# Sorted attention plus routed experts: heads in pairs, a smaller sort matrix, and expert work issued between the attention stages

## The chip, the cores and the metric

One core of one Trainium2 chip. The metric is the device time of one execution in microseconds (us), median over several runs, lower is better.

## The reference, cut to what matters

```python
# attention: batch 4, heads 8, seq 768, head_dim 64, 8 blocks of 96
for _ in range(5):                       # Sinkhorn on sort_net, [32, 8, 8]
    P = exp(P - max);  P /= rows;  P /= columns
k_sorted[i] = sum_j P[i, j] * k_block[j]; v_sorted likewise
attn = softmax(q_block @ k_sorted.T / 8);  o = attn @ v_sorted
x = o as [3072, 512]
# experts: E = 8, D = 512, F = 1024
G = exp(x @ w_gate);  8 Sinkhorn rounds on G [3072, 8]
out = sum_e G[:, e] * (relu(x @ w1[e]) @ w2[e])
```

Every token goes through every expert. That is 8 x 6 chunks of 512 tokens x (32 + 32) matmuls of 512 columns: 3072 in all, in both kernels.

## The kernel before

One head at a time. P goes to memory and comes back spread over the partitions; a sort matrix R of 128 x 2304 is built per head, and twelve matmuls of 384 columns sort k and v together. The expert part comes after the attention.

```python
    Pdr = dram.tile([32, 8, 8], F32)
    nc.sync.dma_start(out=Pdr, in_=P)
    Pbig2 = pp.tile([128, 32, 8], F32)
    for j in range(8):
        nc.gpsimd.dma_start(out=Pbig2[16 * j:16 * (j + 1), :, :], in_=...)      # cut
    ...
    for g in range(NH):                                   # 32 heads
        ktv = iop.tile([128, 6, 128], BF16, name="ktv")   # k | v
        ... three loads, 96 KB each ...
        R = rp.tile([128, 2, 6, 4, 96], BF16, name="R")
        for nh in range(2):
            for i2 in range(4):
                nc.vector.tensor_scalar(out=outap, in0=mask, scalar1=Pbig2[:, g, i:i + 1], ...)
        for nh in range(2):
            for kk in range(6):
                nc.tensor.matmul(sortps[:, nh, 0:384], ktv[:, kk, :], R[:, nh, kk],
                                 start=(kk == 0), stop=(kk == 5))
        ... 8 q transposes, 8 scores, exp, 8 v transposes, 8 products, normalise ...
    ...
    for e in range(E):
        for nc4 in range(6):
            ... 32 matmuls hps, 8 Relu on ACT, 32 matmuls oacc, 4 accumulations on DVE ...
```

The softmax here doesn't subtract the row's maximum and nothing guards it: scores larger than these inputs give would overflow.

## Time and profile before

| | before |
|---|---|
| device time | 852.1 us (848.5 to 855.5, 16 runs) |
| first sort matmul | 27.45 us |
| first expert matmul | 172.9 us |
| last matmul ends | 845.1 us |
| span | 849.3 us |

The four times are read off the timeline: rows give the start, the length, the engine, the source line, the operation with output and inputs, and the idle time before it with what ended it. The page's fourth part and the list of stretches say which of them is on the path. The lines themselves stand in the prediction.

### The profile page before, as it was taken

The page shows a single profiled execution, that of the slowest core. Times are in us where ns is not written, and L with a number is a line of the kernel's source. Part 1 is how long each engine was busy: PE and PEld are TensorE (multiplying, and loading weights), DVE is VectorE, ACT ScalarE, POOL GpSimd, SP SyncE. Part 2 cuts the span into 40 slices and gives each one's busy share as a digit, 9 for nine tenths or more (in the row PEclk, how much of TensorE's full clock was granted, in tenths as well). Part 3 has the DMA queues.
Part 4 walks back from the last instruction along what each step waited for, and adds up shares of the span by engine and source line. Part 5 has one row for each costly group of instructions (what it writes and reads, how often), then busy time and mean ns, then how long its engine had stood idle before and what let it go on. Part 6 is the DMA issues. An engine that isn't in the chain of part 4 may idle for free.

```text
span 849.3 us, 11251 instructions
## 1 busy us (share of the span) xinstructions
PE 797.7 (94%) x4657; PEld 402.4 (47%) x4720; DVE 283.7 (33%) x603; ACT 333.8 (39%) x543; POOL 99.6 (12%) x131
## 2 busy tenths in 40 slices
PE   0678999998999999999999999999999999999997
PEld 0456777753444444444444444444444444444443
DVE  4758888655222222212121212122221212121212
ACT  1357777742333333242424233333324242424332
POOL 4745555300000000000000000000000000000000
PEclk9999999999999999999999999999999999999999
DMA  8999999600006000600060005001400000001212
GB/s 117 124 166 102 71 71 71 44 1 1 1 1 99 1 1 1 100 0 1 1 100 0 1 5 95 0 1 25 75 1 0 1 1 1 0 1 50 100 55 94
DMA packets 92419, 33.52 MB, mean 39 GB/s; under 512 B 76768, under 2 KB 85200, under 8 KB 92368
## 3 DMA queue, kind: packets, MB, share of 16 engines
q0 software_dynamic: 88592, 26.36, 30.2%
q1 hardware_dynamic: 3776, 6.44, 2.1%
q8 instruction: 37, 0.61, 0.3%
q14 instruction: 14, 0.11, 0.1%
HBM read 52.58 MB, written 6.30 MB: 69 GB/s over the span
## 4 chain that ended last, share of the span: by engine, by line
PE 88%; DMA 4%; DVE 3%; ACT 3%; issue 1%; POOL 1%; ACTq 0%
PE oacc L276 39%; PE hps L268 38%; PE sortps L157 7%; ACT kvTs L170 2%; PE tps L191 2%; DMA ktv<-in_k_dram 1%; PE scps L177 1%; DMA ktv<-in_v_dram 1%; PE ogps L201 1%; POOL Pbig L72 1%; DMA Pdr<-P 1%; PE csps L253 0%; DVE cs L252 0%; DMA qg<-in_q_dram 0%; PE ggps L238 0%
## 5 line engine op out<-in xcount | busy, mean ns | idle before, releaser
L271 ACT ACTIVATE hTs<-hps 128x512 bf16<-128x512 f32 x384 | 229.1, 597 | 424.5 <-PE hps L268 404.1
L276 PE MATMUL oacc<-w2e,hTs 128*128 128x512 bf16 x1506 | 339.3, 380 | 3.5 <-DVE osbl L279 1.7
L268 PE MATMUL hps<-xtT,w1e 128*128 128x512 bf16 x1503 | 338.1, 379 | 1.7
L283 DVE SCALAR_TENSOR_TENSOR osbl<-oacc,glog,osbl 128x512 f32<-128x512 f32 x168 | 126.1, 751 | 454.0 <-PE oacc L276 432.4
L276 PEld LDWEIGHTS <-hTs 128*128 128x128 bf16 x1536 | 150.8, 98 | 183.6 <-issue 4.0
L268 PEld LDWEIGHTS <-w1e 128*128 128x128 bf16 x1536 | 150.2, 98 | 179.4
L150 DVE TENSOR_SCALAR R<-mask,Pbig 128x576 bf16<-128x576 bf16 x256 | 92.8, 419 | 21.3 <-DMA Pbig<-Pdr 12.2
L157 PE MATMUL sortps<-R,ktv 128*128 128x384 bf16 x384 | 78.1, 335 | 12.7 <-ACT kvTs L170 6.4
L103 POOL DMA_DIRECT2D w1e<-in_moe_w_dram x8 | 6.1, 762 | 399.1 <-PE hps L268 399.1
L157 PEld LDWEIGHTS <-ktv 128*128 128x128 bf16 x384 | 35.1, 100 | 34.0 <-issue 11.9
L166 PE MATMUL tps<-I,qg 96*96 96x96 bf16 x256 | 17.5, 211 | 26.9 <-DMA qg<-in_q_dram 26.9
L170 ACT CAST kvTs<-sortps 128x768 bf16<-128x768 f32 x32 | 25.5, 798 | 41.2 <-PE sortps L157 41.2
L279 DVE TENSOR_SCALAR osbl<-oacc,glog 128x512 f32<-128x512 f32 x24 | 17.8, 750 | 46.9 <-PE oacc L276 45.4
L184 ACT ACTIVATE atp<-scps 96x768 bf16<-96x768 f32 x32 | 25.8, 806 | 19.4 <-PE scps L177 18.3
L140 POOL DMA_DIRECT2D ktv<-in_k_dram x32 | 26.7, 835 | 55.2 <-PE sortps L157 43.6
L166 PEld LDWEIGHTS <-qg 96*96 96x96 bf16 x256 | 15.7, 127 | 28.1 <-issue 27.0
L141 POOL DMA_DIRECT2D ktv<-in_v_dram x32 | 26.4, 826 | 0.0
L142 POOL DMA_DIRECT2D qg<-in_q_dram x32 | 25.9, 809 | 0.1
L172 ACT COPY qTs<-tps 96x768 bf16<-96x768 bf16 x32 | 25.5, 795 | 0.1
L208 DVE TENSOR_TENSOR ogallP<-ogps,recips 96x512 bf16<-96x512 f32 x32 | 21.7, 678 | 0.3
L177 PEld LDWEIGHTS <-kvTs 96*96 96x96 bf16 x256 | 16.8, 126 | 4.7 <-issue 0.8
L195 ACT COPY vsbP<-tps 96x512 bf16<-96x512 bf16 x32 | 18.3, 573 | 0.0
(47 smaller groups left out, 174.0 us busy)
## 6 DMA issues: line engine op xcount, KB each, us to landing
w1e<-in_moe_w_dram POOLq DMA_DIRECT2D x8, 1024.0 KB, 8.1
w2e<-in_moe_w_dram POOLq DMA_DIRECT2D x8, 1024.0 KB, 8.9
out_dram<-osbl SPq DMA_DIRECT2D x24, 256.0 KB, 2.0
ktv<-in_k_dram POOLq DMA_DIRECT2D x32, 96.0 KB, 3.1
ktv<-in_v_dram POOLq DMA_DIRECT2D x32, 96.0 KB, 3.7
qg<-in_q_dram POOLq DMA_DIRECT2D x32, 96.0 KB, 3.5
Pbig<-Pdr POOLq DMA_DIRECT2D x8, 16.0 KB, 2.4
mask<-mask SPq DMA_DIRECT2D x7, 18.0 KB, 5.3
```

Of the source, the lines that this page charges most:

```text
L140: nc.gpsimd.dma_start(out=ktv[:, :, 0:64], in_=kf[g].rearrange("(p kk) d -> p kk d", kk=6))
L141: nc.gpsimd.dma_start(out=ktv[:, :, 64:128], in_=vf[g].rearrange("(p kk) d -> p kk d", kk=6))
L142: nc.gpsimd.dma_start(out=qg[0:96, qb, :, 0:64], in_=qf[g].rearrange("i c d -> c i d"))
L150: nc.vector.tensor_scalar(out=outap, in0=mask, scalar1=Pbig2[:, g, i:i + 1], scalar2=None, op0=ALU.mult)
L157: nc.tensor.matmul(sortps[:, nh, 0:384], ktv[:, kk, :], R[:, nh, kk], start=(kk == 0), stop=(kk == 5),)
L166: nc.tensor.matmul(qTps[0:96, i, :], qg[0:96, qb, i, :], I96, is_transpose=True, start=True, stop=True)
L170: nc.scalar.copy(kvTs, sortps[:, :, 0:384])
L184: nc.scalar.activation(out=atp[0:96], in_=scps[0:96, :, 0:384], func=AF.Exp, scale=scale)
L268: nc.tensor.matmul(hps, w1e[:, kk, fb * 128:(fb + 1) * 128], xtT[:, kk, nc4 * 512:(nc4 + 1) * 512], start=(kk == 0), stop=(kk == 3))
L271: nc.scalar.activation(out=hTs[:, fb, :], in_=hps, func=AF.Relu)
L276: nc.tensor.matmul(oacc, hTs[:, fb, tt * 128:(tt + 1) * 128], w2e[:, fb, :], start=(fb == 0), stop=(fb == 7))
L283: nc.vector.scalar_tensor_tensor(out=osbl[:, t, :], in0=oacc, scalar=glog[:, t, e:e + 1], in1=osbl[:, t, :], op0=ALU.mult, op1=ALU.add)
```

## The change

Its intent: get rid of the trip to memory, make the attention cheap on TensorE, and hand the time that TensorE still idles in it to expert matmuls. Cut to its core:

```diff
-    Pdr = dram.tile([32, 8, 8], F32)                      # P out and back, eight loads
-    ...
+    for _ in range(46):                                   # dummy matmuls, to have the clock up
+        nc.tensor.matmul(w_, wide[:, 0:128], wide, start=True, stop=True)
+    ... Sinkhorn with one max instead of five; the last product writes Prep, P repeated 16 times ...
+    for i in range(8):
+        nc.tensor.matmul(pbp[:, i, :], Prep[:, i]..., ident[0:32, 0:32], start=True, stop=True)
+    def stage1(m):                                        # pair m of heads
+        for src, dic, nm in ((kb, KT, "KT"), (vb, VT, "VT")):
+            for kh2 in range(2):
+                b_ = bank([128, 3, 128])
+                for k3 in range(3):
+                    for h2 in range(2):                   # head 0 -> partitions 0-63, head 1 -> 64-127
+                        nc.tensor.matmul(b_[64 * h2:64 * h2 + 64, k3, :], src[:, h2, 3 * kh2 + k3, :],
+                                         R[:, h2]..., start=True, stop=True)
+                ... KT halves and the first VT half copied by ACT, the second by DVE ...
+        ... 12 q transposes likewise, QT copied by DVE; R of the next pair built (256 columns) ...
+    ... stage2: 16 scores of 64 rows, exp, 8 transposes to VS; stage3: 16 products, normalise;
+        stage4: 8 transposes, copied into xtT by ACT ...
+    for m in range(NPAIR + 4):                            # order of every engine's queue as written
+        stage1(m); fill(1); stage2(m - 1); fill(1); stage3(m - 2); fill(1); gate; stage4(m - 3); fill(1)
+    ... routing rounds with fill(3) each; then y tiles, h blocks up to nine chunks ahead ...
```

`fill(1)` issues one expert block (four matmuls of 512 columns and a Relu), if the batch it needs is through the attention. All PSUM tiles rotate through one pool of eight banks.

## The prediction

> **What bounds the kernel now.** I read the stretches first, cut where the tenths of the engines change. Columns: stretch, length, then busy time and instruction count of PE, PEld, DVE, ACT and POOL, granted TensorE clock, DMA share, GB/s.
>
> ```profile
> 0.00:23.73 23.73, 0.00 (x0) 0.00 (x0) 9.12 (x42) 2.56 (x6) 11.31 (x24) 1.00 0.78 107
> ...
> 80.00:160.00 80.00, 75.00 (x908) 56.76 (x907) 67.52 (x190) 59.03 (x85) 46.45 (x57) 1.00 1.12 72
> ...
> 204.36:849.30 644.94, 637.64 (x2905) 290.13 (x2963) 141.90 (x189) 219.55 (x368) 8.18 (x10) 1.00 0.13 27
> ```
>
> Three quarters of the span is the expert network, TensorE 99% busy. Before it come 24 us without a matmul, then attention at a fixed beat: 57 POOL issues at three a head are 19 heads in 80 us, 4.21 us a head. No expert matmul runs in that stretch.
>
> The chain that ended last, in order of time (start, length, what), gives the speed of the expert part and the cause of the empty start.
>
> ```profile
> 13.84 4.61 DMA Pdr<-P
> 18.73 5.00 POOL Pbig L72 x8
> ...
> 810.57 6.91 PE oacc L276 x32
> ```
>
> Thirty-two 512-column matmuls take 6.91 us, 215.9 ns each. The experts need 3072 of them: 8 experts x 6 chunks x (32 + 32). That is **663.2 us, untouched by the change**. The timeline has the first expert matmul at 172.9 and the end of the last at 845.1: 672.2 us, of which 9 are stalls around the routing iterations. The last 4.2 us are the last DVE instruction and the last store. So 849.3 = 27.4 (first sort matmul) + 145.5 (attention) + 663.2 + 9 + 4.2. The first two terms and the 9 can be won.
>
> TensorE's timeline in the attention shows what small matmuls cost.
>
> ```profile
> 102.57 0.52 PE L177 MATMUL scps<-qTs,kvTs 96*96 96x96 bf16 x8
> 103.02 0.54 PE L191 MATMUL tps<-Ibig,kvTs 64*96 64x64 bf16 x8
> 103.50 1.31 PE L157 MATMUL sortps<-R,ktv 128*128 128x384 bf16 x7
> 104.64 0.51 PE L201 MATMUL ogps<-vsbP,atp 96*96 96x65 bf16 x8
> 104.99 0.33 PE L157 MATMUL sortps<-R,ktv 128*128 128x384 bf16 x1
> ```
>
> A group's busy time runs to the modelled end of its last matmul, some 0.21 us long, so the starts count: L201's eight take 0.35 us, 44 ns each. Sort matmuls start 163 ns apart (1.14 us for seven), so twelve cost 1.95 us: almost half of a head. The rest (0.45 + 0.48 + 0.35 + 0.37, and a quarter of four groups of 0.39) makes about 4.0 of the 4.21 us. TensorE bounds the attention too, with DVE close behind at 84%.
>
> **What the Trainium skill says.**
> (1) "TensorE: Matmul & The Clock Gate", section "Back-to-back issue gap": a warm matmul of N columns takes N/2.4 + 2.5 ns. That gives 215.8 for 512 and 162.5 for 384; the trace agrees (215.9, 163).
> (2) "TensorEngine Tiling (Array Packing)", section "Key Properties": tiles of the array can work in parallel, and changing the tiling mode drains the engine. The second half shows here: L191 uses 64 rows, its last start is about 0.33 us after its first, yet the next group starts at 0.48, a gap of 0.15 where 0.05 is usual. I charge 0.1 us a change of mode. No run of before shows two tiles in parallel.
> (3) "VectorE: DVE Perf Modes", section on mode 1x: PSUM operands work at one element a cycle of 0.96 GHz. The trace agrees: ogallP, 512 elements out of PSUM, took 678 ns, which is 533 + 145.
> (4) "ScalarE: Activation LUTs", "What ACT_TABLE_LOAD costs": 186 + 0.833 N ns. The trace is slightly below: 597 ns for 512, 798 for 768.
>
> **The change part by part.**
> *Start.* P no longer goes out to memory and back through eight issues; eight small matmuls and one copy spread it. Sinkhorn loses a maximum and a subtraction in four of five rounds, 4 x 0.48 = 1.9 us, so its end moves from 13.8 to about 11.9; the widened last product (1024 elements, 1.2 us against 0.26), the matmuls (0.8), the copy (0.4) and the first R (0.4) put the first sort matmul at about **15 us** instead of 27.4. The 46 dummy matmuls fit: about ten at the cold 0.43 us (the before trace shows that spacing from 203 to 206 us) and 36 at 0.216 are 12.1 us from about 1.5.
>
> *Attention on TensorE.* Heads go in pairs, and R shrinks: the sort multiplies by a 128-column block structure instead of a 384-column one accumulated six times. Per pair: 36 matmuls of 128 columns at 56 ns (2.02 us), 16 scores of 96 at 46 (0.74), 8 transposes of 128 at 56 (0.45), 16 of 65 columns at 44 (0.70), 8 of 96 at 49 (0.39): 4.3 us a pair against 8.4. Four changes of mode add 0.4; running the two 64-column halves in parallel may win back as much or more, so I leave 4.3. Sixteen pairs: **69 us**, with 2.4 for the gate (96 at 25 ns, as before).
>
> *Attention on DVE and ACT, per pair.* DVE at elements/0.96 + 0.15 to 0.2 us: VT half 0.58, QT 0.95, R 0.42, VS 1.22, four times reciprocal and product (0.20 + 0.41) 2.44: 5.6, and 13 gaps of 0.04 make **6.1**. ACT at the measured line (about 0.49 for 384): seven of those and one of 0.80, 4.3. With four expert blocks between the stages, half of whose Relus go to DVE (0.75 each), DVE has 7.7, ACT 5.5, and TensorE 4.3 + 4 x 0.864 + 0.15 = 7.9.
>
> *Step by step.* Blocks may fill only once a batch's four pairs are through. Rounds 0 to 2 fill the pipe: DVE's queue puts their end at about 29.5 us. Rounds 3 to 6 have no fill and go at DVE's 6.1: to 54. Nine rounds (7 to 15) with fill are nearly balanced between TensorE and DVE; I take 8.4 for in-order waits: to 129.5. The four draining rounds are TensorE's own 6.2 + 4.6 + 4.0 + 3.7: to 148. By then 52 of 384 blocks (45 us) are done. Routing: eight rounds of DVE's chain, which before repeats every 2.97 us and loses the 0.24 of ACT's scaling: 2.8 against three blocks and the small matmul (2.7), 22.4 in all: to 170.5, with 76 blocks done. Left are 3072 - 304 = 2768 matmuls at 215.9 ns: 597.6 us. One us for the last glog and 4.2 for the tail: **773 us of span**. By sum: 15 + 69 + 2.4 + 663.2 + 1 (column sums) + 17 (DVE stalls in the attention) + 2 + 4.2 = 774. Device times lie 2 to 3 us above the span (852.1 against 849.3), so **776 us**: 9% less.
>
> *Buffers and weights.* Ten hT tiles carry expert work done ahead: 76 blocks are 9.5 tiles, so nothing blocks. Two weight buffers instead of three: w1 of the third expert is asked for after the second y chunk and needed about two chunks (28 us) later, and a load lands in 8 to 9 us. At the end y runs nine chunks alone, 256 KB of output every 1.73 us, 152 GB/s; the stores' queue moved 6.44 MB in 2.1% of 849 us, about 360 GB/s, so only the last store shows.
>
> **Rivals.**
> *A: the loads bound the early attention.* Nothing hides 0.59 MB (as bf16) a pair plus a 1.05 MB weight load in the first rounds: 5.2 MB by round 6 at 47 us, 110 GB/s. For it: before waits 3.66 us at 45 to 49 us for a k tile. Against: that was at 180 GB/s, in small pieces; the new layout writes 768 bytes a run instead of 128. If it held, the early rounds take 7 to 8 us: 785.
> *B: the array's halves run in parallel and DVE hardly waits.* A pair takes 3.2 us of TensorE, filled rounds fall to 7.5: 764 to 768. Nothing of before speaks for or against.
> *C: TensorE gets cold or stops and starts.* Rounds 0 to 6 leave it idle a third of the time. Before went at half speed from 201.8 to 206 after a gap of 1.7 us. With small matmuls at half speed early, and eight banks turned over by in-order queues, each round costs 1.5 us more: 795.
> *D: the expert part itself slows*, because order is now fixed by hand: 1% of it is 6.6 us. Against: the old order ran at 215.9 ns for 2900 matmuls with three banks a side; now there are eight.
>
> **Range and chances.** The 663 are certain to within a few us, so the range is that of the 110 us left: B at its best gives 757, A or C with hiccups in the filled rounds 797. To fall within 2% (835) the whole attention gain would have to go; I see nothing that does that. Faster 0.97, same 0.02, slower 0.01.
>
> **What would show it right or wrong.** First sort matmul at 15 us (12 to 17); expert matmuls at 216 ns throughout; DVE over 90% busy in the rounds before the first expert block, at about 6 us a pair; 8 to 8.5 us a pair after it; routing done at about 170 us, with TensorE over 95% busy in it. It would be wrong if k, v or q loads stand among the longest waits of TensorE, if the clock is under 0.9 for more than 10 us after the start, or if expert matmuls wait for weights or for DVE after 170 us.

## The result

**746.9 us** (746.3 to 747.4, 8 runs) against 852.1: the ratio is 0.8765, 95% interval 0.8751 to 0.8779. (Ratios here are the mean time of one kernel's runs over that of the other's of the same rounds, so not quite the ratio of the medians.) The direction was right and the gain was 105 us where 76 were forecast; 746.9 lies 10 us below the low end of the range.

The stretches of the kernel after, cut at the first sort matmul, the start of the first round with expert blocks, near the last of those, and around the routing. Columns as in the prediction.

```profile
14.45:39.01 24.56, 21.29 (x508) 19.13 (x508) 21.42 (x61) 20.18 (x48) 14.93 (x22) 1.00 1.30 203
39.01:102.00 62.99, 61.61 (x953) 41.45 (x970) 49.30 (x132) 42.43 (x93) 12.29 (x17) 1.00 0.68 111
...
120.00:143.00 23.00, 22.89 (x115) 10.95 (x116) 16.09 (x47) 14.56 (x26) 0.00 (x0) 1.00 0.00 1
143.00:744.60 601.60, 594.53 (x2713) 270.63 (x2766) 144.70 (x194) 184.31 (x309) 9.79 (x12) 1.00 0.16 32
```

From 39 us on TensorE is busy 98% or more. DVE is at 78% in the filled rounds (49.3 of 63), where the prediction had it nearly even with TensorE. The chain that ended last still has P's last product and the first sort matmul at the start, but nothing from memory between them:

```profile
11.84 1.23 DVE Prep L130
14.45 0.88 PE bank L164 x24
```

TensorE's timeline in a filled round, to set beside the small matmuls of before:

```profile
88.54 0.53 PE L164 MATMUL bank<-R,kb 128*64 128x128 bf16 x12
88.90 0.50 PE L164 MATMUL bank<-R,vb 128*64 128x128 bf16 x12
89.24 0.50 PE L175 MATMUL bank<-ident,qb 128*64 128x128 bf16 x12
89.67 1.04 PE L241 MATMUL bank<-xtT,w1e 128*128 128x512 bf16 x3
90.64 0.56 PE L190 MATMUL bank<-QT,KT 64*96 64x96 bf16 x16
91.12 0.65 PE L197 MATMUL bank<-ident,VT 128*96 128x128 bf16 x8
```

Go by the starts: twelve 128-column matmuls take 0.36 and 0.34 us, 28 to 30 ns each on average, half of the 56 that the prediction charged. Sixteen scores take 0.48 us. A group hides how its members start. A window that opens late in one shows only the members still running then; here the last four and the last three q transposes of the round before:

```profile
82.66 0.28 PE L175 MATMUL bank<-ident,qb 128*64 128x128 bf16 x4
82.66 0.28 PE L175 MATMUL bank<-ident,qb 128*64 128x128 bf16 x3
```

They start in pairs, one for each half of the array: 3 to 4 ns between the two of a pair and 56 ns from pair to pair (single starts at 82.655, 82.659, 82.711 and 82.715).

DVE's groups up to 102 us (busy, mean ns of one, idle before):

```profile
L213 DVE TENSOR_TENSOR OG<-bank,rc 96x256 bf16<-96x256 f32 x56 | 23.6, 421 | 1.9
...
L200 DVE COPY vs<-bank 96x1024 bf16<-96x1024 bf16 x15 | 10.3, 690 | 2.9 <-PE bank L197 2.9
...
L178 DVE COPY QT<-bank 128x768 bf16<-128x768 bf16 x16 | 8.7, 546 | 0.0
```

The fp32 product came out as worked (0.41 predicted, 0.42). The two bf16 copies did not: 0.69 instead of 1.22, 0.55 instead of 0.95.

The prediction's schedule beside the trace (starts of the first sort matmul of a round, from the timeline; span, us. Round 16 has none: its start is the expert group at 101.79 us plus one block of 0.86. Routing likewise: the last gate's end and one block.):

| milestone | predicted | after | miss of this step |
|---|---|---|---|
| first sort matmul | 15 | 14.45 | 0.5 |
| round 3 starts | 29.5 | 22.05 | 6.9 |
| round 7 starts (expert blocks from here) | 54 | 39.01 | 7.5 |
| round 16 starts | 129.5 | 102.7 | 11.8 |
| routing starts | 148 | 120.7 | 0.5 |
| first y matmul | 170.5 | 142.9 | 0.3 |
| end (170.5 + 597.6 + 1 + 4.2) | 773.3 | 744.6 | 1.1 |

So 26 of the 29 us lie between the first sort matmul and round 16. Start, draining rounds, routing and experts were right within 1.5 us each. The experiments look for the causes of those 26, and for what the large gain is made of.

### The profile page after: what moved, and what is told of

It reads as the page before. It is cut to its first block, busy times and chain, and to the rows that moved or that the text cites.

```text
span 744.6 us, 10572 instructions
## 1 busy us (share of the span) xinstructions
PE 730.3 (98%) x4503; PEld 357.6 (48%) x4582; DVE 251.8 (34%) x497; ACT 273.9 (37%) x497; POOL 48.9 (7%) x71
## 4 chain that ended last, share of the span: by engine, by line
PE 95%; DVE 2%; ACT 1%; issue 1%; DMA 0%; ACTq 0%
PE bank L327 44%; PE bank L241 44%; PE bank L164 2%; PE bank L209 1%; PE bank L197 1%; PE bank L190 1%; PE bank L220 1%; PE bank L175 1%; ACT xtT L222 0%; ACT at L193 0%; PE bank L229 0%; DMA P<-in_sort_net_dram 0%; PE bank L310 0%; DVE rs L124 0%; ACT P L119 0%
## 5 line engine op out<-in xcount | busy, mean ns | idle before, releaser
L247 ACT ACTIVATE hTs<-bank 128x512 bf16<-128x512 f32 x358 | 213.7, 597 | 371.2 <-PE bank L241 363.2
L241 PE MATMUL bank<-xtT,w1e 128*128 128x512 bf16 x1490 | 341.9, 379 | 2.0
L327 PE MATMUL bank<-w2e,hTs 128*128 128x512 bf16 x1503 | 336.0, 379 | 1.7
L333 DVE SCALAR_TENSOR_TENSOR osbl<-bank,glog,osbl 128x512 f32<-128x512 f32 x168 | 126.1, 751 | 398.8 <-PE bank L327 386.0
L330 DVE TENSOR_SCALAR osbl<-bank,glog 128x512 f32<-128x512 f32 x24 | 18.0, 750 | 54.7 <-PE bank L327 51.7
L193 ACT ACTIVATE at<-bank 96x384 bf16<-96x384 f32 x64 | 26.0, 491 | 8.3 <-PE bank L190 8.3
L213 DVE TENSOR_TENSOR OG<-bank,rc 96x256 bf16<-96x256 f32 x64 | 26.9, 421 | 2.2
L245 DVE TENSOR_SCALAR hTs<-bank 128x512 bf16<-128x512 f32 x26 | 17.7, 682 | 6.1 <-PE bank L241 6.1
L209 PEld LDWEIGHTS <-at 96*96 96x96 bf16 x256 | 13.9, 125 | 2.4
L209 PE MATMUL bank<-vs,at 96*96 96x65 bf16 x256 | 14.2, 209 | 0.0
L111 PE MATMUL bank<-wide 128*128 128x512 bf16 x46 | 11.7, 421 | 1.2 <-DVE wide L63 1.2
L212 DVE RECIPROCAL rc<-bank 96x4 f32<-96x4 f32 x64 | 10.9, 171 | 3.8 <-PE bank L209 3.8
```

Of the source, the lines that this page charges most:

```text
L193: nc.scalar.activation(out=ATT[m][h2][:, half, :], in_=bb[h2].rearrange("k i q -> k (i q)"), func=AF.Exp, scale=scale)
L209: nc.tensor.matmul(b_[:, i4, :], ATT[m][h2][:, half, 96 * i4:96 * i4 + 96], VS[m][:, i, h2, :], start=True, stop=True)
L213: nc.vector.tensor_tensor(out=OG[m][:, 4 * half:4 * half + 4, h2, :], in0=b_[:, :, 0:64], in1=mkap(rc, [rc.ap[0], [1, 4], [0, 64]]), op=AL ...
L241: nc.tensor.matmul(b_, w1t[e][:, kk, fb * 128:(fb + 1) * 128], xf[:, kk, c * 512:(c + 1) * 512], start=(kk == 0), stop=(kk == 3))
L245: nc.vector.tensor_scalar_max(hT[e, c][:, fb, :], b_, 0.0)
L247: nc.scalar.activation(out=hT[e, c][:, fb, :], in_=b_, func=AF.Relu)
```

## The experiments

**Undoing the alternation between the halves of the array.**

```diff
-            for kh2 in range(2):
-                b_ = bank([128, 3, 128])
-                for k3 in range(3):
-                    for h2 in range(2):
+            two = [bank([128, 3, 128]) for _ in range(2)]
+            for h2 in range(2):
+                for kh2 in range(2):
+                    for k3 in range(3):
```

(the q transposes and the scores likewise)

> The changed kernel with one thing undone: matmuls of the two heads of a pair no longer alternate between the two halves of the array; all those of head 0 of a tile come first, then those of head 1. Same instructions, same number. Theory T (two tiles of the array work in parallel, which is why twelve 128-column matmuls start within 0.34 us): the twelve take about 0.57 us, a pair costs TensorE 0.75 us more, the nine filled rounds go from 6.8 to 7.6 us, and the time rises by 7 to 9 us, to 754 to 756. Rival N (a matmul with 64 stationary columns is simply short, 28 ns, in any order): twelve still take 0.34 us and the time stays at 747 within 1.

Measured: 749.1 us, 2.2 more. Filled rounds take 6.98 instead of 6.80 us. By the letter this is neither theory: close to N, but the trace says why. Single starts in this kernel's TensorE timeline:

```profile
84.21 0.22 PE L164 MATMUL bank<-R,vb 128*64 128x128 bf16 x1
84.24 0.22 PE L164 MATMUL bank<-R,kb 128*64 128x128 bf16 x1
84.26 0.22 PE L164 MATMUL bank<-R,vb 128*64 128x128 bf16 x1
84.29 0.22 PE L164 MATMUL bank<-R,kb 128*64 128x128 bf16 x1
```

In the program all twelve kb matmuls come before the first vb matmul. Its first vb matmuls are those of head 0, the last kb matmuls those of head 1. Here they start in turns: the two halves run their own matmuls side by side, several instructions apart. Reordering did not separate them, so the experiment missed its aim and another was needed.

At the end of the stage, though, only head 1 has matmuls left. The last three, two and one q transposes (windows that open late, as above):

```profile
84.85 0.33 PE L177 MATMUL bank<-ident,qb 128*64 128x128 bf16 x3
84.91 0.28 PE L177 MATMUL bank<-ident,qb 128*64 128x128 bf16 x2
84.96 0.22 PE L177 MATMUL bank<-ident,qb 128*64 128x128 bf16 x1
```

A half that works alone starts one every 56 ns. So a narrow matmul is not short, and rival N falls by this trace; while both halves have work, each keeps its own 56 ns and the two together give one every 28.

**Doubling two DVE copies.**

```diff
         nc.vector.tensor_copy(QT[m], b_)
+        nc.vector.tensor_copy(QT[m], b_)
...
         nc.vector.tensor_copy(VS[m][:, :, :, 0:64], b_.rearrange("c i (h d) -> c i h d", d=64))
+        nc.vector.tensor_copy(VS[m][:, :, :, 0:64], b_.rearrange("c i (h d) -> c i h d", d=64))
```

> The changed kernel with the copies of QT and VS out of PSUM made twice on DVE: 0.55 + 0.69 = 1.24 us more a pair, about what the prediction had charged these two copies too much (0.93) plus its gaps. Theory D (DVE sets the beat of the rounds without expert blocks, and its bf16 copies being short is the second half of the missed gain): rounds 2 to 6 go from about 4.2 to 5.4 us, 6 to 7 us in all; the filled rounds, with DVE at 6.5 of 6.8, lose 0 to 2; 753 to 756. Rival (TensorE, ACT or the banks set that beat): within 2 us of 747.

Measured: 755.0 us, 8.1 more, inside the expectation of theory D. Rounds 4 to 7 start 5.35 us apart. The stretch of three rounds without expert blocks in this kernel, and then in the kernel after:

```profile
29.55:45.61 16.06, 11.99 (x252) 10.00 (x252) 15.45 (x43) 11.16 (x25) 8.75 (x13) 1.00 1.25 205
```

```profile
25.86:39.01 13.15, 11.16 (x254) 10.07 (x253) 12.41 (x39) 10.71 (x24) 8.84 (x13) 1.00 1.31 201
```

DVE (third pair of numbers) is at 96% with the copies doubled and at 94% without. DVE's cost matters where there are no expert blocks. Whether it also set the beat of the kernel after is not shown by this: a dearer engine can take over a bound.

**Both of the former.**

> Both of the former: no alternation between halves, and the two copies made twice. It sets the kernel to the two costs that the prediction had assumed. If the two account for the miss (28 us by the prediction's own schedule), the time goes to 765 to 776. If they only add up as in the two single runs: 761 to 765, and some 10 us of the miss are from the prediction's allowance for in-order waits and gaps.

Measured: 759.1 us. It lies below both expectations. As the first part did not separate the halves, this run says nothing on the account. It is 1.9 us above the sum of the two single runs (2.2 and 8.1 more); in its rounds at 41 to 49 us TensorE waits 0.45 and 0.60 us on copies by ACT, which was not followed up.

**No expert blocks inside the attention.**

```diff
     def fill(n, both=True):
+        if both:
+            return
```

> The changed kernel without expert blocks inside the attention rounds (the routing rounds keep theirs). Theory I (interleaving gains what TensorE would idle in the rounds bound by DVE and ACT): rounds 7 to 15 then go at 4.4 us with TensorE needing 3.3, so about nine rounds lose 1 us each, and the draining rounds another 1 to 2: 755 to 758. Rival (the expert work that was moved forward only displaces attention work, since TensorE is full either way): 747 to 749.

Measured: 762.1 us, 15.2 more: theory I, but larger than expected. By the starts of rounds, rounds 7 to 14 lose 7.6 us (with 27.6 us of expert work taken off), round 15 with the draining rounds 6.0, the routing 1.6. The expectation had missed how long the pipe drains when nothing else fills it. It had also missed the clock: in the thin draining rounds the granted clock fell, to 0.59 from 85 to 90 us and 0.73 from 90 to 95, and the first twelve expert matmuls took 3.92 us where twelve take 2.59 at full clock. So most of the 1.6 of the routing (1.3) is the clock, and some of the 6.0 may be. TensorE's timeline in a round of the attention shows the waits that expert blocks cover otherwise:

```profile
70.87 0.53 PE L164 MATMUL bank<-R,kb 128*64 128x128 bf16 x12
71.83 0.53 PE L164 MATMUL bank<-R,vb 128*64 128x128 bf16 x12 [0.43 <-ACT xtT L222]
72.21 0.53 PE L175 MATMUL bank<-ident,qb 128*64 128x128 bf16 x12
72.67 0.69 PE L190 MATMUL bank<-QT,KT 64*96 64x96 bf16 x16
73.67 0.61 PE L197 MATMUL bank<-ident,VT 128*96 128x128 bf16 x8 [0.32 <-ACT at L193]
```

**The whole array for the same number of matmuls** (wrong result).

```diff
-    nc.tensor.matmul(b_[64 * h2:64 * h2 + 64, k3, :], src[:, h2, 3 * kh2 + k3, :],
+    nc.tensor.matmul(b_[:, k3, :], src[:, h2].rearrange("p kk d -> p (kk d)")[:, at(3 * kh2 + k3)],
...
-    hs = slice(64 * h2, 64 * h2 + 64)
+    hs = slice(0, 128)
```

(`at(kk)` is a window of 128 columns; the q transposes likewise.)

> Wrong result on purpose. The changed kernel with the same number of matmuls, but none in a part of the array: the 36 of the first stage take 128 stationary columns and write all 128 partitions, the 16 scores take all 128 rows. Reordering (the first run of this study) did not keep the two halves apart, since starts interleave over the halves whatever the order; this does. Theory T (parallel halves): twelve 128-column matmuls take 0.67 us instead of 0.34, the scores 0.70 instead of 0.48; a pair costs TensorE about 1.0 us more after the changes of mode that fall away; filled rounds 6.8 to 7.8 (plus 9 us in all), rounds without fill plus 0 to 0.5 each: 757 to 760. Rival N (narrow matmuls are simply short, and parallel work of halves plays no part): wide ones may be slower too, so N would only be kept if the twelve stayed near 0.34 us: 747.

Measured: 757.2 us, 10.3 more, as theory T expected. Filled rounds take 7.68 us, 0.88 more. Its TensorE timeline in a filled round:

```profile
81.97 0.83 PE L167 MATMUL bank<-R,kb 128*128 128x128 bf16 x12
82.64 0.83 PE L167 MATMUL bank<-R,vb 128*128 128x128 bf16 x12
83.31 0.83 PE L178 MATMUL bank<-ident,qb 128*128 128x128 bf16 x12
83.98 1.03 PE L244 MATMUL bank<-xtT,w1e 128*128 128x512 bf16 x3
84.84 0.88 PE L193 MATMUL bank<-QT,KT 128*96 128x96 bf16 x16
```

Twelve now take 0.67 us, 56 ns each, double. This run alone would leave open whether a narrow matmul is merely short; with the lone half of the first experiment at 56 ns and the starts in pairs, the parallel halves are shown, and this run gives what they are worth.

**Whole array and doubled copies** (wrong result).

> Wrong result on purpose. The former together with the two DVE copies made twice: both costs that the prediction assumed, in one kernel. Rounds without fill as with the copies alone (5.4 us), filled rounds at TensorE's 7.8 with DVE at 6.5: the sum of the two single runs, plus 8 and plus 11, gives 765 to 767. If the two costs explain the miss fully (prediction's schedule 776), 770 or more.

Measured: 763.5 us, 16.6 more. Somewhat less than the sum of the single runs (8.1 + 10.3 = 18.4), and well short of the prediction's 776. The two mis-sized costs explain 17 of the 29 us (if anything less, as doubling adds 1.24 us a pair where the prediction charged 0.93 too much). The other 12 are elsewhere, and this run's rounds tell where: with about the costs that the prediction assumed, the nine filled rounds take 7.91 us on average with the gate in, where it took 8.4, and a round without fill 5.3 where it took 6.1.

**The start alone, in the kernel before.**

```diff
-    Pdr = dram.tile([32, 8, 8], F32)          # and the store, the eight loads
+    nc.vector.tensor_copy(Prep, mkap(P, [P.ap[0], [8, 8], [1, 8], [0, 16]]))
+    for i in range(8):
+        nc.tensor.matmul(pbp[:, i, :], Prep[:, i]..., Ibig[0:32, 0:32], start=True, stop=True)
+    nc.vector.tensor_copy(Pbig2.rearrange("p g i -> p i g"), pbp)
```

> The kernel before with one part of the change alone: P is spread over the partitions by eight small matmuls and a copy instead of a trip to memory and eight loads. First sort matmul at about 15 us instead of 27.4. If nothing else binds early: 12 us less, 840. If the early loads bind (before has TensorE waiting for k and v tiles between 45 and 60 us): 843 to 848.

Measured: 840.7 us against 852.4, 11.7 less by the medians (ratio 0.9878, 0.9842 to 0.9913, so 7 to 13 us): the first expectation, in time. In detail it was not met: the first sort matmul came at 18.88, not 15, after waiting for a v tile.

```profile
14.54 0.39 PE L74 MATMUL pbp<-Ibig,Prep 32*128 32x32 bf16 x8 [14.54 <-DVE Prep L69]
18.88 3.86 PE L157 MATMUL sortps<-R,ktv 128*128 128x384 bf16 x12 [3.96 <-DMA ktv<-in_v_dram]
```

So the start moved by 8.6 us only. In the two profiled executions (spans 849.3 and 839.3) the first expert matmul comes 7.8 us earlier, at 165.1 for 172.9, and another 1.7 comes after it: before has TensorE at half speed from 201.8 to 206 us (clock 0.60), and this execution has no such spell (clock 1.00 from 165 to 200). By these traces the start is worth about 8 us; the rest is that spell and the spread between executions.

**No dummy matmuls.**

```diff
-    for _ in range(46):
-        nc.tensor.matmul(w_, wide[:, 0:128], wide, start=True, stop=True)
```

> The changed kernel without the 46 dummy matmuls of the start. If they only bring the clock up, the first one or two rounds run at half clock, twice 1 to 2 us more: 748 to 750. If the rounds without fill are too thin to bring the clock up by themselves, all seven go at half clock: 755 or more. If the start did not need them: 746 to 747.

Measured: 748.6 us, 1.7 more, as the first theory said. Two rounds ran at half speed:

```profile
14.32 0.85 PE L161 MATMUL bank<-R,kb 128*64 128x128 bf16 x12 [0.97 <-DVE R L146]
...
17.43 0.85 PE L161 MATMUL bank<-R,kb 128*64 128x128 bf16 x12 [0.98 <-DVE R L146]
...
21.10 0.53 PE L161 MATMUL bank<-R,kb 128*64 128x128 bf16 x12
```

Twelve matmuls take 0.60 us to the next group in the first two rounds and 0.36 in the third. In this run the rounds without fill are dense enough to bring the clock up and keep it up (the GpSimd run below shows that it can fall there).

**Attempts at a better kernel, which also ask what sets 4.39 us.** First, q transposes of three pairs before P is ready (40 dummy matmuls instead of 46, copies by ACT):

```diff
+    for m in range(3):
+        make_qt(m, nc.scalar.copy)       # 12 transposes and a copy, before the spread of P
     pbp = bank([128, 8, 32])
```

> An attempt at a better kernel, and a test of what sets the beat of the rounds without expert blocks. The Q transposes of the first three pairs are made before P is ready, on an idle TensorE, and copied by ACT, which idles there; DVE loses 0.55 us in each of three early rounds. Theory D (DVE sets that beat): up to 3 x 0.5 = 1.5 us less, 745.4 to 746.4. If ACT or bank waits set it, or the third q load lands late and holds the queue up: 746.5 to 749.

Measured: 749.6 us, worse by 2.7 and above even the last expectation. The third q load landed late and held the queue, and P's spread behind it, up:

```profile
14.65 0.53 PE L140 MATMUL bank<-ident,qb 128*64 128x128 bf16 x12 [1.56 <-DMA qb<-in_q_dram]
15.11 0.36 PE L149 MATMUL bank<-ident,Prep 32*128 32x32 bf16 x8
16.45 0.85 PE L179 MATMUL bank<-R,kb 128*64 128x128 bf16 x12 [0.98 <-DVE R L164]
```

The clock had fallen as well (0.85 us for the twelve).

Second, R built by GpSimd:

```diff
-        nc.vector.tensor_tensor(
+        (nc.gpsimd if m else nc.vector).tensor_tensor(     # R, two rounds ahead
```

> The same question from another side: R (0.41 us of DVE a round) is built by GpSimd two rounds ahead, from the second pair on. Theory D: rounds without fill from 4.39 to about 4.0 us, five of them, 2 us less: 744.5 to 745.5; the filled rounds, bound by TensorE, do not change. Against: GpSimd issues the loads too (2.2 us a round), and R may come late: 747 to 752.

Measured: 746.9 us, no gain. The profiled execution is the slowest of the four (748.2): after a gap of 1.30 us TensorE works at half speed from about 28 to 35 us (clock 0.63 from 31.40 to 36.44). So it has just one undisturbed steady round, which takes 4.37 us (36.44 to 40.81 us in the timeline) with 0.41 us of DVE work gone. The next run, with R on GpSimd too, has three, of 4.04, 4.38 and 4.37. None of its other executions (746.5 at best) reached theory D's 745.5. So DVE alone does not set 4.39 in the kernel after: theory D falls for it, though DVE does set the beat once it has 1.24 us more.

Third, both:

> Both of the former. Theory D: 3 us less than the changed kernel, 743.5 to 744.5, with ACT (3.65 us a round) next in line. If either part goes wrong, as bad as the worse of the two.

Measured: 748.2 us, between the two: the late load again (TensorE waits 2.29 us for the third q tile), and the clock at 0.50 from 17 to 21.5 us.

Fourth, two evacuations swapped between ACT and DVE:

```diff
-                if nm == "KT" or kh2 == 0:
-                    nc.scalar.copy(dst, b_)
-                else:
-                    nc.vector.tensor_copy(dst, b_)
+                nc.scalar.copy(dst, b_)
...
-        nc.scalar.copy(xtT[:, hpi, b]..., b_...)
+        nc.vector.tensor_copy(xtT[:, hpi, b]..., b_...)
```

> The changed kernel with two evacuations swapped: the copy into xtT (768 bf16 out of PSUM, 0.80 us on ACT) goes to DVE, where bf16 copies take 0.55, and the second VT half (fp32, 0.55 on DVE) to ACT at 0.49. DVE's work stays the same, ACT loses 0.3 us a round. Theory L (the 4.39 us beat of the rounds without expert blocks is a loop through TensorE and ACT: the V matmuls wait 0.43 us for the xtT copy, the VT transposes 0.32 for the exponentials): the first wait goes, 4.39 falls to 4.0 to 4.2, five rounds, 745 to 746. Theory D (DVE sets it, at 4.2 us of work): 4.39 stays, 747. If the copy now waits in DVE's queue behind the products of two pairs: 748 or more.

Measured: 746.5 us. Rounds of 4.07 to 4.19 us, as theory L said, so the wait for xtT was a part of the loop. The 745 to 746 was not reached. But a shorter wait on another ACT copy takes its place, and 0.2 us in five rounds is not told apart from the kernel after in time (746.9, other chip and rounds):

```profile
30.61 0.33 PE L164 MATMUL bank<-R,vb 128*64 128x128 bf16 x6
31.23 0.36 PE L164 MATMUL bank<-R,vb 128*64 128x128 bf16 x6 [0.29 <-ACT KT L168]
```

Fifth, that with R on GpSimd:

> The former with R built by GpSimd, so that DVE has 3.76 us of work a round, ACT 3.35 and TensorE 3.3. Theory L: no engine is near the beat, 3.6 to 4.0 us a round, 744 to 745. If the eight banks and the order of the queues keep a loop of their own: 4.2 to 4.4 us as in all variants so far, 746 to 747.

Measured: 746.2 us; rounds of 4.13 to 4.43 us, although by the trace DVE has 3.76 and ACT 3.25 us of work in one, and TensorE's attention takes 3.35 in a filled round. Its rival held: some loop of in-order queues and eight banks stays near 4.2 us. Which link of it is the last one was not settled.

No version tried is clearly faster than the kernel after. All variants except the two that are wrong gave correct results.

## Why the prediction was wrong

Its structure held. The experts' 663 us stood, the first sort matmul came at 14.45 (15 said), the draining rounds, the routing and the tail were right, loads did not bind (rival A), the clock stayed at 1.00 (rival C), the expert part kept its speed (rival D). The chance of 0.97 for faster was right. The size was off by 29 us, from terms of one sum:

1. **"36 matmuls of 128 columns at 56 ns (2.02 us), 16 scores of 96 at 46 (0.74)"** and "so I leave 4.3". The halves run in parallel: a sort matmul costs 28 ns, and a pair of scores 45. That takes 1.01 + 0.36 = 1.37 us off a pair of heads. The prediction wrote that parallel halves "may win back as much or more" than four changes of mode at 0.1, and then counted "as much". The 0.1 was right (0.09 and 0.10 in the trace of after); 4.3 + 0.4 - 1.37 would have given 3.33. A filled round holds 16 x 0.216 = 3.45 us of expert matmuls, so of 6.80 us the attention takes 3.35, where 4.3 was charged. With the whole array it takes 7.68 - 3.45 = 4.23, which is the prediction's figure: the count and the durations were right for a TensorE without parallel tiles. The trial that takes the parallelism away costs 10.3 us. The prediction had this as rival B, and its 3.2 us a pair is close to the 3.35 measured. But it let B's filled round fall to 7.5 only, near the 7.7 that its own sum gives DVE, which is the next term's error, and so B ended at 764 to 768 (757 "at its best").

2. **"QT 0.95 ... VS 1.22"**, one element a cycle. They took 0.55 and 0.69: 768 elements in 400 ns plus 146, 1024 in 533 plus 157, two elements a cycle of 0.96 GHz. The prediction had cited the page's mode 1x and read it as the rule for anything in PSUM; that section says only that PSUM operands work in this mode. The 678 ns of ogallP, offered as agreement, are of an fp32 operand. Two sections on, the same page says in "Why PSUM operands drop a tier" that PSUM caps at the packed two-element mode and only fp32 at one. The trace of before had no bf16 copy from PSUM on DVE to correct this (ACT made those), so here the page had to be read to the end. Doubling these copies costs 8.1 us, and with term 1 together 16.6.

3. **"13 gaps of 0.04"** and **"I take 8.4 for in-order waits"**. Independent DVE instructions leave no gap; their records overlap. The DVE timeline of a filled round of the kernel after:

```profile
62.17 0.55 DVE L178 COPY QT<-bank 128x768 bf16<-128x768 bf16 x1
62.64 0.42 DVE L149 TENSOR_TENSOR R<-Pbig,mask 128x256 bf16<-128x256 f32 x1
62.97 0.68 DVE L245 TENSOR_SCALAR hTs<-bank 128x512 bf16<-128x512 f32 x1
```

R starts 0.08 us before QT's record ends. The 0.04 is the gap in before's Sinkhorn chain (5.64 to 5.68 us), where each instruction needs the last one's result. Before's own R group had shown it: 92.8 us busy for 256 instructions of 419 ns, 363 each. And the in-order waits did not come: with the prediction's own costs (the run with the whole array and doubled copies) filled rounds run at 7.68 us plus the gate every fourth, 7.91 on average and so TensorE's own sum of 7.9, where 0.5 was added; rounds without fill at 5.3, not 6.1. That is 0.5 us in nine rounds, 0.8 in four, and 3 in the first three (11.5 us to round 3 in that run, 14.5 predicted): some 10.5 of the 12 us that the two first terms leave. Another 1 is in the step from span to device time: the prediction set the median 852.1 against the span of an execution of 851.1. What is left is within the small misses of the table's other steps.

The prediction's "DVE over 90% busy in the rounds before the first expert block" was seen (94%), and still was not the cause: relieving DVE left 4.04 to 4.38 us. A busy engine close to the beat is not yet the one that sets it.

Where the 105 us come from, as far as runs show it: the start is worth about 8 in the kernel before (11.7 by the medians), the expert blocks inside the attention 15.2, the parallel halves 10.3. These were taken in different kernels and need not add up. The largest piece was not isolated; by arithmetic it is the sort itself, 32 x 12 matmuls at 163 ns (62.6 us) against 16 x 24 at 28 ns (10.9 us), an estimate from the two timelines, and it holds part of those 10.3.

## What to carry to other kernels

Where two heads or blocks each need only half of the array, put them on different partitions of the output (or rows of the input) and issue them next to each other: here twelve matmuls went from 0.67 to 0.34 us, and the order within a dozen hardly mattered (0.18 us in a filled round). Give a latency-bound stage independent matmuls to run between its steps; it paid 15 us here, 6 of it in the draining rounds that no steady-state estimate shows and 1.6 in the routing, most of it because the clock had fallen without them. When predicting, take gaps from independent instructions rather than from a dependent chain, don't add an allowance for waits that no trace shows, and read a page to its end.

## What the Trainium skill lacked or had wrong

- "TensorE: Matmul & The Clock Gate", Part 3, "The mechanism", says that matmuls start and end strictly in program order. The first experiment shows starts out of it between two column halves: vb of head 0 at 84.21 us, before kb of head 1 at 84.24 and 84.29, which precedes it in the program.
- "TensorEngine Tiling (Array Packing)", "Theoretical Speedup" gives up to 2x for 64 columns. It was reached here: twelve in 0.34 us against 0.67. The page has no figure for the drain at a change of mode. In the trace of after, the first full-array matmul starts 0.151 us after the last q transpose, where 0.056 is usual, and the VT transposes 0.135 after the last score, where pairs of scores start 0.045 apart: 0.09 to 0.10 us a change. With it, sixteen 64-row scores of 96 columns gain only 1.5x, 0.48 against 0.72 us (84.84 to 85.56 in the whole-array run).
- "VectorE: DVE Perf Modes", "Why PSUM operands drop a tier", is right, but its mode 1x section names PSUM operands without that limit. Measured: bf16 copies out of PSUM of 768 elements in 546 ns and 1024 in 690; fp32, 384 elements in 553.
- "VectorE: DVE Perf Modes", "The DRAIN you can't avoid", has the next operation wait until the pipe is empty, but adds that one which is not held starts earlier. Here the exception is the usual case: in the records, independent neighbours overlap by about 0.08 us (62.64 against 62.72), so durations must not simply be added.
